# Batch 0 of a fused attention and feed-forward kernel in another layout of the accumulation banks

## Chip, cores and metric

The kernel runs on one core of a Trainium2 chip. The metric is device time in microseconds (us) of one execution. Lower is better. The time before is the median of seven executions.

The core has a matrix engine (TensorE, PE in the profile), a vector engine (VectorE, DVE), a scalar engine (ScalarE, ACT), a general engine (GpSimd, POOL) and an engine that here only issues transfers (SyncE, SP). PE writes its products into eight accumulation banks of 2 KB per partition (PSUM); DVE and ACT carry them from there to the working memory.

## Reference

```python
B, H, S, D = q.shape                     # 8, 8, 576, 64
q_d = q.reshape(B, H, S // 4, 4, D).mean(axis=3)     # k_d, v_d the same
out_up = np.repeat(sm_attn(q_d, k_d, v_d), 4, axis=2)        # full attention over 144 positions
mask = np.abs(pos[:, None] - pos[None, :]) < 4
out_local = softmax(where(mask, 0.125 * q @ k.T, -1e9)) @ v  # a band of seven keys
x = (out_up + out_local).transpose(0, 2, 1, 3).reshape(B * S, H * D)   # 4608 x 512
h = x @ w_in                                                  # 512 x 2048
g = np.where(h > 0, h, np.exp(np.minimum(h, 0)) - 1)
return g @ w_out                                              # 2048 x 512, result fp32
```

## The kernel before, in words

Each batch has eight heads, treated as four pairs (`j` = 0 to 3). The feed-forward part runs over nine blocks `t` of 512 tokens: 16 first products of four matmuls each (`mm1.t.fc`), the activation in three steps (`e` on ACT, `m` and `g` on DVE), and 16 pieces of four matmuls of the second product (`mm2.t.i`), four pieces to a bank that ACT copies out (`oc`) and SP stores (`st`). A block needs the attention output of one or two batches.

Nothing is scheduled by a compiler. The string `ORDER` (lines 40 to 148) lists some 1,500 words; each word calls a function, and every engine executes its instructions in the order in which the words stand. So a word that must wait holds up all later words of its engine. The words that matter here:

- `Lq`, `Lk`, `Lv` load a pair's q, k, v on SP's queue (lines 309, 319), into ten staging buffers; `Cq`, `Ck`, `Cv` cast them to fp16 on POOL (373, 381). `Dq`, `Dk` load and cast two pairs in one transfer on POOL's queue (339), `WI` and `WO` a quarter of the weights (269, 274). `WL` (`hold`, 296) is a one-element write on POOL into a staging buffer: SP's next load waits for it, and with it for everything POOL has to do first.
- `Tq`, `Tk` turn q and k (`turn`; for batches 0 to 2 in 18 matmuls of 64 columns, line 408). `Aq`, `Ak` carry the turned tile away (434; ACT, and DVE for k of pairs 0 and 1 of batch 0); `Fq`, `Fk` add up fours on DVE (453).
- `SL` is the banded part of the scores (504), `SD` the pooled part (514); `SC` is both. `G0`, `G1` and `H0`, `H1` are the exponentials of the two parts on ACT (530, 536), one for each head; `E0`, `E1` are both. `M` multiplies with the band's mask on DVE (549).
- `VS` pools v (391) and `VD` carries that away on DVE (478). `DH` (batch 0, two halves) and `DEN` make the denominators (573); `RH` and `RC` invert them (583, 587).
- `OUT` makes a pair's output (624, 630), `LG` carries it to the working memory on ACT (645, 648), `RB` spreads the inverted denominators by ten matmuls with a selector (613), `MUL` multiplies the two on DVE (657, 660), `X` adds the two parts into the block's input, on POOL but for one on DVE (673).
- `Z` and `FILL` put matmuls of 512 columns on constant data into the next tile before its real work (254).
- `K?` loads constants; `KS` loads the selector `SEL`, 128 x 1280 fp16, on POOL's queue (211).

Until the word `Q0` only batch 0 is computed. The eight banks are then two double-bank tiles with the tag `two` and two with the tag `more`. All turns, the v sums (but one), the first half's denominators, the outputs and the spread use `two` in rotation; the scores, one v sum, the second half's denominators and one spread use `more`. A tile is handed on when its last reader is done. `SL` and `SD` of one head share a tile: the pooled scores lie behind the banded ones in the same banks (columns 288 to 431). At `Q0` the banks of `more` are given to the feed-forward part, as two banks `hp` and two banks `misc`.

Of the kernel before, what the change touches and what calls it, by code (L numbers as in the profile page):

```python
# [15 lines left out]
SD = S // 4  # L16
# [34 lines left out]
Lv1.3 e.0.2 SC1.0 e.0.1 Fk1.1 Cv1.0 mm1.0.4 E01.0 m.0.2 g.0.2 WO2 e.0.3 VS1.0 E11.0 m.0.1
mm1.0.6 VD1.0 WO3 g.0.1 e.0.4 SC1.1 WLv2.0 M1.0 e.0.6 mm1.0.9 E01.1 m.0.4 g.0.4 E11.1 m.0.6
OUT1.0 g.0.6 mm1.0.15 LG1.0 M1.1 Tq1.3 m.0.3 Tq1.2 g.0.3 Aq1.3 Dq2.1 mm1.0.14 Aq1.2 Fq1.3 Tk1.2
e.0.15 Fq1.2 mm1.0.7 e.0.14 m.0.15 Lv2.0 Ak1.2 g.0.15 Cv1.1 Tk1.3 e.0.7 Fk1.2 Dk2.1 mm1.0.8
Ak1.3 m.0.7 e.0.9 g.0.7 SC1.2 Fk1.3 E01.2 m.0.14 g.0.14 E11.2 VS1.1 m.0.9 mm1.0.13 VD1.1 e.0.8
M1.2 SC1.3 e.0.13 m.0.8 g.0.9 E01.3 m.0.13 mm1.0.5 g.0.13 E11.3 g.0.8 OUT1.1 e.0.5 M1.3 mm1.0.11
LG1.1 m.0.5 g.0.5 Tq2.0 e.0.11 Tq2.1 Cv1.2 Lv2.1 Aq2.0 mm1.0.12 Aq2.1 m.0.11 g.0.11 VS1.2 e.0.12
Tk2.0 VD1.2 mm2.0.0 Fq2.1 Ak2.0 Fq2.0 Tk2.1 OUT1.2 Fk2.0 Ak2.1 mm2.0.1 LG1.2 m.0.12 g.0.12
mm1.0.10 Fk2.1 DEN1 e.0.10 m.0.10 SC2.1 g.0.10 E02.1 RC1 mm2.0.2 E12.1 RB1.2 mm2.0.3 MUL1.2
Cv1.3 Lv2.2 RB1.1 oc.0.0 M2.1 VS1.3 st.0.0 mm2.0.4 MUL1.1 X1.2.2 X1.2.1 mm2.0.5 VD1.3 X1.1.2  # L60
X1.1.1 RB1.0 OUT1.3 MUL1.0 mm2.0.6 LG1.3 X1.0.2 Lv2.3 RB1.3 X1.0.1 Tq2.2 MUL1.3 mm2.0.7 Aq2.2
Cv2.0 Fq2.2 Tk2.2 X1.3.2 Lq3.0 oc.0.1 X1.3.1 VS2.0 Ak2.2 mm2.0.8 st.0.1 VD2.0 Cv2.1 Fk2.2 SC2.0
Lk3.0 Cv2.2 mm2.0.9 E02.0 mm2.0.10 E12.0 Tq2.3 M2.0 Tk2.3 Lv3.0 Aq2.3 mm1.1.0 Cv2.3 Ak2.3 Fq2.3
mm1.1.3 e.1.0 Fk2.3 Cq3.0 Lq3.1 SC2.2 e.1.3 m.1.0 mm2.0.11 E02.2 g.1.0 m.1.3 mm2.0.12 E12.2
g.1.3 Ck3.0 Lk3.1 mm1.1.1 oc.0.2 M2.2 st.0.2 mm1.1.4 e.1.1 m.1.1 Lv3.1 VS2.3 e.1.4 g.1.1 Cv3.0
OUT2.0 mm2.0.13 VD2.3 LG2.0 m.1.4 g.1.4 Cq3.1 Lq3.2 mm1.1.6 mm1.1.11 e.1.6 Ck3.1 Lk3.2 SC2.3
e.1.11 mm2.0.14 m.1.6 E02.3 g.1.6 mm2.0.15 m.1.11 E12.3 g.1.11 mm1.1.2 Cv3.1 Lv3.2 oc.0.3 st.0.3
mm1.1.5 M2.3 e.1.2 m.1.2 VS2.2 Lq3.3 e.1.5 g.1.2 OUT2.3 DEN2 VD2.2 LG2.3 m.1.5 g.1.5 mm1.1.9
Lk3.3 RC2 mm2.1.0 e.1.9 m.1.9 mm1.1.7 Lv3.3 g.1.9 Cv3.2 VS2.1 e.1.7 mm1.1.10 VD2.1 m.1.7 g.1.7
OUT2.1 e.1.10 Lq4.0 RB2.1 LG2.1 m.1.10 mm1.1.15 g.1.10 MUL2.1 RB2.0 e.1.15 Lk4.0 mm1.1.13 MUL2.0  # L70
X2.1.2 RB2.3 e.1.13 m.1.15 mm2.1.1 g.1.15 X2.0.2 Lv4.0 MUL2.3 OUT2.2 X2.0.3 mm1.1.8 X2.1.3 LG2.2
m.1.13 Lq4.1 g.1.13 X2.3.2 RB2.2 e.1.8 Tq3.0 MUL2.2 X2.3.3 Cv3.3 mm1.1.14 Aq3.0 m.1.8 Tk3.0
VD3.0 X2.2.2 e.1.14 g.1.8 Ak3.0 Tq3.1 X2.2.3 mm1.1.12 KD3.0 Cq3.2 Aq3.1 m.1.14 mm2.1.2 Lk4.1
e.1.12 g.1.14 Cq3.3 Tq3.2 VD3.1 Cv4.0 mm1.2.0 Aq3.2 m.1.12 g.1.12 Cq4.1 Tk3.1 e.2.0 VD3.2 Ck3.3
# [24 lines left out]
MUL4.0 mm1.3.15 X4.3.4 Lq6.3 m.3.12 SC5.2 e.3.15 g.3.12 X4.0.4 mm2.3.2 E05.2 Cv6.1 mm1.4.0 E15.2
m.3.15 g.3.15 Cv6.2 Tq5.3 e.4.0 M5.2 mm1.4.2 Aq5.3 m.4.0 g.4.0 Cq6.2 Tk5.3 e.4.2 mm2.3.3 VD5.3  # L100
X4.0.5 Ak5.3 mm1.4.3 m.4.2 oc.3.0 g.4.2 Ck6.2 st.3.0 Tq6.2 KD5.3 e.4.3 Cq6.1 mm1.4.10 Aq6.2
m.4.3 g.4.3 Cq6.0 Tk6.2 e.4.10 mm2.3.4 VD6.2 X4.3.5 Ak6.2 Lk6.3 mm2.3.5 m.4.10 g.4.10 Cv6.0
mm1.4.5 KD6.2 SC5.3 e.4.5 mm1.4.7 E05.3 m.4.5 g.4.5 mm2.3.6 E15.3 mm1.4.12 e.4.7 M5.3 SC6.2
m.4.7 e.4.12 g.4.7 DEN5 E06.2 m.4.12 g.4.12 mm1.4.14 E16.2 RC5 mm1.4.13 SO5 M6.2 e.4.14 Tq6.1
e.4.13 m.4.14 g.4.14 Tq6.0 Aq6.1 Cq6.3 mm2.3.7 Aq6.0 m.4.13 VD6.1 mm1.4.1 g.4.13 oc.3.1 VD6.0
st.3.1 Tk6.1 e.4.1 mm1.4.15 Ck6.3 SI5 mm2.3.8 m.4.1 g.4.1 Ck6.0 e.4.15 mm2.3.9 Ak6.1 Lv6.3
m.4.15 Tk6.0 g.4.15 Lq7.0 mm1.4.9 Ak6.0 Lk7.0 KD6.1 mm1.4.8 KD6.0 e.4.9 m.4.9 SC6.1 e.4.8 g.4.9
mm2.3.10 E06.1 m.4.8 g.4.8 mm1.4.4 E16.1 mm1.4.11 e.4.4 M6.1 SC6.0 m.4.4 e.4.11 g.4.4 mm2.3.11
E06.0 m.4.11 Lv7.0 g.4.11 mm2.3.12 E16.0 OUT5.1 oc.3.2 M6.0 Lq7.1 OUT5.2 st.3.2 MUL5.1 Cv6.3
mm2.3.13 Cq7.0 MUL5.2 mm1.4.6 Lk7.1 X5.1.5 OUT5.3 X5.1.6 e.4.6 OUT5.0 MUL5.3 mm2.3.14 X5.2.5  # L110
Lv7.1 X5.2.6 MUL5.0 mm2.3.15 X5.3.6 Tq6.3 Lq7.2 oc.3.3 m.4.6 g.4.6 X5.0.5 Tk6.3 Aq6.3 st.3.3
mm2.4.0 X5.0.6 Ak6.3 VD6.3 mm2.4.1 X5.3.5 KD6.3 Cv7.0 Lk7.2 SC6.3 Ck7.1 mm1.5.0 E06.3 Cq7.1
mm1.5.8 E16.3 Lv7.2 Cv7.1 Tq7.0 e.5.0 M6.3 e.5.8 Tq7.1 m.5.0 Aq7.0 Lq7.3 g.5.0 Ck7.0 DEN6 Aq7.1
# [37 lines left out]
def _np_consts():  # L151
# [15 lines left out]
    for e in range(2):  # L167
        for g in range(RN):
            sel[:, RN * e + g, g, e] = 1.0
# [640 lines left out]
```

## Time and profile before

| | |
|---|---|
| median of 7 runs | 364.0 us (362.22 to 367.38) |
| profiled execution, its own time | 366.4 us |
| its span, first to last instruction | 364.6 us |
| PE busy | 350.4 us (96% of the span) |
| DVE, ACT, POOL busy | 241.1, 208.9, 122.0 us |
| mm1 matmuls (line 681), 576 of 128 x 512 | 144.4 us busy |
| mm2 matmuls (line 725), 576 of 128 x 512 | 142.0 us busy |

The profile is of one execution, and the other six have only a time. A busy PE is not PE at its peak: a matmul's row is longer than the step from one matmul to the next. Four 128 x 512 matmuls in a row step on by 0.86 us on the chain, 0.22 us each. Where the timeline merges a group, its duration runs from the first start to the last end, and a group may begin before the one ahead of it has ended. "issue" is idle time for which the profile shows no event that ended it.

### The profile page before, as it was taken

The page shows a single profiled execution, that of the slowest core. Times are in us where ns is not written, and L with a number is a line of the kernel's source. Part 1 is how long each engine was busy: PE and PEld are TensorE (multiplying, and loading weights), DVE is VectorE, ACT ScalarE, POOL GpSimd, SP SyncE. Part 2 cuts the span into 40 slices and gives each one's busy share as a digit, 9 for nine tenths or more (in the row PEclk, how much of TensorE's full clock was granted, in tenths as well). Part 3 has the DMA queues.
Part 4 walks back from the last instruction along what each step waited for, and adds up shares of the span by engine and source line. Part 5 has one row for each costly group of instructions (what it writes and reads, how often), then busy time and mean ns, then how long its engine had stood idle before and what let it go on. Part 6 is the DMA issues. An engine that isn't in the chain of part 4 may idle for free.

```text
span 364.6 us, 9565 instructions
## 1 busy us (share of the span) xinstructions
PE 350.4 (96%) x3960; PEld 184.4 (51%) x3960; DVE 241.1 (66%) x473; ACT 208.9 (57%) x395; POOL 122.0 (33%) x177
## 2 busy tenths in 40 slices
PE   7898978999999998999999999999999999999995
PEld 3664544554565463565555655645544444444442
DVE  2878985577887575658797875868666655555520
ACT  2757884277567785376767775674743344444421
POOL 5777211562195150652193219506001400000000
PEclk9999999899999999999999999999999999999999
DMA  8999999598997998666952399940013010010012
GB/s 269 209 188 200 197 197 197 111 164 171 206 169 151 166 173 166 119 138 125 191 106 61 78 190 221 147 133 31 29 53 91 30 59 29 29 60 29 29 60 86
DMA packets 106918, 46.10 MB, mean 126 GB/s; under 512 B 92314, under 2 KB 101178, under 8 KB 106874
## 3 DMA queue, kind: packets, MB, share of 16 engines
q1 hardware_dynamic: 96586, 34.61, 47.4%
q0 software_dynamic: 6576, 6.96, 11.2%
q10 hardware_dynamic: 3712, 3.93, 5.1%
q8 instruction: 31, 0.51, 0.6%
q14 instruction: 13, 0.11, 0.1%
HBM read 42.50 MB, written 9.53 MB: 143 GB/s over the span
## 4 chain that ended last, share of the span: by engine, by line
PE 79%; DMA 14%; POOL 2%; SPq 1%; DVE 1%; ACT 1%; issue 1%; ACTq 0%
PE op L725 34%; PE hp L681 30%; DMA v<-in_v_dram 10%; PE sc L504 3%; PE lg L624 2%; DMA rd<-rc 2%; PE den L573 2%; PE tq L391 2%; PE tq L414 2%; DMA q<-in_q_dram 1%; PE tk L414 1%; PE rb L613 1%; PE lg L630 1%; SPq L319 1%; POOL WI L269 1%; POOL v L381 1%
## 5 line engine op out<-in xcount | busy, mean ns | idle before, releaser
L681 PE MATMUL hp<-xt,WI 128*128 128x512 f16 x576 | 144.4, 380 | 0.2
L725 PE MATMUL op<-WO,gt 128*128 128x512 f16 x576 | 142.0, 382 | 1.1 <-DVE gt L715 1.1
L706 ACT ACTIVATE e<-hp 128x512 f16<-128x512 f32 x144 | 85.6, 600 | 80.5 <-PE hp L681 74.7
L715 DVE SCALAR_TENSOR_TENSOR gt<-hp,e 128x512 f16<-128x512 f32 x144 | 99.1, 690 | 4.8
L725 PEld LDWEIGHTS <-gt 128*128 128x128 f16 x576 | 53.5, 98 | 62.6 <-DVE gt L715 1.6
L710 DVE TENSOR_SCALAR e<-e 128x512 f16<-128x512 f16 x144 | 49.7, 345 | 52.0 <-ACT e L706 50.5
L681 PEld LDWEIGHTS <-WI 128*128 128x128 f16 x576 | 52.9, 98 | 59.3 <-issue 0.9
L673 POOL TENSOR_TENSOR xt<-ln,gn 128x64 f16<-128x64 f16 (+7 forms) x63 | 42.3, 695 | 62.4 <-DVE ln L660 62.3
L530 ACT ACTIVATE pex<-sc 112x576 f16<-112x576 f32 x64 | 41.0, 647 | 10.9 <-PE sc L514 8.5
L381 POOL CAST v<-v 112x768 f16<-112x768 f32 x30 | 25.4, 855 | 49.3 <-DMA v<-in_v_dram 27.1
L732 ACT COPY os<-op 128x512 f32<-128x512 f32 x36 | 21.1, 586 | 31.3 <-PE op L725 30.8
L549 DVE TENSOR_TENSOR mex<-pex,MASK 112x1152 f16<-112x1152 f16 x32 | 27.6, 862 | 17.0 <-ACT pex L530 16.8
L536 ACT ACTIVATE dex<-sc 72x288 f16<-72x288 f32 x64 | 25.5, 405 | 1.3 <-PE sc L514 1.3
L376 POOL CAST k<-k 96x768 f16<-96x768 f32 x20 | 16.6, 837 | 26.0 <-issue 12.6
L376 POOL CAST q<-q 96x768 f16<-96x768 f32 x20 | 17.6, 887 | 20.4 <-issue 14.8
L504 PEld LDWEIGHTS <-kt 64*112 64x112 f16 x384 | 12.9, 127 | 14.2 <-issue 11.4
L504 PE MATMUL sc<-qt,kt 64*112 64x96 f16 x384 | 17.1, 218 | 2.0 <-issue 1.3
L439 ACT CAST qt<-tq 128x720 f16<-128x720 f32 x20 | 15.0, 763 | 5.7 <-PE tq L391 3.1
L391 PEld LDWEIGHTS <-VR 112*72 112x72 f16 x192 | 13.1, 115 | 6.3 <-issue 2.7
L660 DVE TENSOR_TENSOR ln<-lg,rcb 128x576 f16<-128x576 f32 x20 | 14.9, 747 | 0.0
L624 PEld LDWEIGHTS <-v 112*64 112x64 f16 x384 | 10.6, 109 | 7.7 <-issue 5.9
L624 PE MATMUL lg<-mex,v 112*64 112x96 f16 x384 | 13.7, 209 | 0.6 <-ACT lg L648 0.3
(65 smaller groups left out, 271.8 us busy)
## 6 DMA issues: line engine op xcount, KB each, us to landing
v<-in_v_dram SPq DMA_DIRECT2D x28, 336.0 KB, 6.8
out_dram<-os SPq DMA_DIRECT2D x36, 256.0 KB, 2.3
q<-in_q_dram SPq DMA_DIRECT2D x24, 288.0 KB, 6.2
k<-in_k_dram SPq DMA_DIRECT2D x24, 288.0 KB, 5.8
rcb<-rd ACTq DMA_DIRECT2D x10, 360.0 KB, 6.2
WI<-in_moe_w_in_dram POOLq DMA_DIRECT2D x4, 512.0 KB, 10.7
WO<-in_moe_w_out_dram POOLq DMA_DIRECT2D x4, 512.0 KB, 15.7
q<-in_q_dram POOLq DMA_DIRECT2D x4, 288.0 KB, 11.6
```

Of the source, the lines that this page charges most:

```text
L376: nc.gpsimd.tensor_copy(out=t, in_=x.rearrange("p (e c d) -> p c e d", e=2, d=D))
L381: nc.gpsimd.tensor_copy(out=t[:], in_=st32.pop(("v", b, j)).rearrange("p (e c) d -> p c e d", e=2))
L504: nc.tensor.matmul(sc[e][0:KW, c // 3, QB * (c % 3) : QB * (c % 3) + QB], kt[r, QB * c : QB * c + KW], q_of(b, j, r, c), start=True, stop= ...
L530: nc.scalar.activation(out=stS[(b, j)][2][:, e, :].rearrange("p (g u) -> p g u", g=2), in_=scs[(b, j)][e][0:KW, :, 0:HB], func=AF.Exp, sca ...
L549: nc.vector.tensor_tensor(out=mex[:], in0=pex[:], in1=mk2, op=AB.mult)
L624: nc.tensor.matmul(lg[64 * e : 64 * e + 64, c // 3, QB * (c % 3) : QB * (c % 3) + QB], v16[:, c, e, :], mex[:, e, QB * c : QB * c + QB], s ...
L673: eng.tensor_tensor(out=xts[t][:, j, t0 - TBLK * t : t1 - TBLK * t], in0=ln[:, a:z], in1=_rep4(gn[:, a // 4 : z // 4]), op=AB.add,)
L681: nc.tensor.matmul(hps[(t, fc)][:], WI[:, dc, 128 * fc : 128 * fc + 128], xts[t][:, dc, :], start=(dc == 0), stop=(dc == DMC - 1),)
L706: nc.scalar.activation(out=e[:], in_=hps[(t, fc)][:], func=AF.Exp)
L710: nc.vector.tensor_scalar(out=e[:], in0=e[:], scalar1=1.0, scalar2=-1.0, op0=AB.min, op1=AB.add)
L715: nc.vector.scalar_tensor_tensor(out=gts[t][:, fc, :], in0=hps[(t, fc)][:], scalar=0.0, op0=AB.max, in1=els.pop((t, fc))[:], op1=AB.add,)
L725: nc.tensor.matmul(ops[(t, tt)][:], gts[t][:, fc, 128 * tt : 128 * tt + 128], WO[:, fc, :], start=(fc == 0), stop=(fc == FCN - 1),)
```

## The change

The banks of batch 0 are laid out anew. In place of two double-bank tiles `more` there are four single banks with the tag `t`. Turns of batch 0 go there as fp16 (a turned pair, 576 values, then fits one bank), made with the matrix engine's transpose flag; so do the v sums, the pooled scores (each head in a bank of its own, no longer behind the banded scores) and both halves of the denominators. The double-bank tiles `two` hold the banded scores, the outputs and the spread alone.

The selector is loaded as 128 x 20 values as the first constant on POOL's queue, and the new word `KX` widens it to 128 x 1280 with two DVE copies that read each value 64 times. Before, it was loaded whole, with the word `KS` standing behind `Ck0.3`.

`ORDER` is written anew as a whole. All its words are the same but for `KX` and the `Z` words, which now stand for 21 filling matmuls in place of 20.

```diff
-RB_MORE = ((0, 2),)
+RB_MORE = ()
 ORDER = """
-KM Lq0.0 KV TBL Lk0.0 FILL Lq0.1 KN Lk0.1 KE Lq0.2 KI Lk0.2 Cq0.0 Ck0.0 Lq0.3 Tq0.0 Lk0.3 Aq0.0
-Tk0.0 Cq0.1 Lv0.0 Ak0.0 Ck0.1 Lv0.1 Z2 Tq0.1 Fq0.0 Lv0.2 SL0.0 Cq0.2 Aq0.1 Fk0.0 Ck0.2 Tk0.1
-G00.0 Z2 Tq0.2 Cq0.3 Ak0.1 G10.0 Fq0.1 Aq0.2 Ck0.3 SD0.0 Tk0.2 H00.0 Fk0.1 KS H10.0 Ak0.2 M0.0
-SL0.1 Z3 Tq0.3 Fq0.2 G00.1 Cv0.0 Lv0.3 G10.1 Fk0.2 Z3 VS0.0 Aq0.3 M0.1 Fq0.3 SD0.1 Tk0.3 Cv0.1
-H00.1 H10.1 Dq1.0 Ak0.3 SL0.2 Fk0.3 WI0 G00.2 G10.2 VD0.0 Dk1.0 Z2 VS0.1 M0.2 Cv0.2 SD0.2 VD0.1
-DH0.0 H00.2 H10.2 WI1 VS0.2 RH0.0 WI2 SL0.3 VD0.2 Z2 OUT0.0 G00.3 WI3 G10.3 RB0.0 WLv1.0 LG0.0
-Lv1.0 M0.3 SD0.3 Lv1.1 H00.3 Cv0.3 Lv1.2 MUL0.0 OUT0.1 H10.3 Z1 DH0.1 LG0.1 X0.0.1 X0.0.0 VS0.3
-RH0.1 RB0.1 VD0.3 Z2 OUT0.2 MUL0.1 Z1 RB0.2 LG0.2 X0.1.0 OUT0.3 MUL0.2 Z2 RB0.3 LG0.3 X0.1.1 Q0
...
+KM Lq0.0 KS KE Lk0.0 FILL TBL Lq0.1 KV Lk0.1 Lq0.2 KN Lk0.2 KI Cq0.0 KX Ck0.0 Lq0.3 Tq0.0 Lk0.3
+Aq0.0 Tk0.0 Cq0.1 Lv0.0 Lv0.1 Ak0.0 Z2 Tq0.1 Ck0.1 Lv0.2 Fq0.0 SL0.0 Cq0.2 Aq0.1 Fk0.0 Fq0.1
+Ck0.2 Tk0.1 G00.0 Z2 Tq0.2 Ak0.1 Cq0.3 G10.0 SD0.0 Fk0.1 Aq0.2 Tk0.2 Ck0.3 SL0.1 H00.0 Fq0.2
+Ak0.2 Z3 Tq0.3 M0.0 H10.0 G00.1 SD0.1 Fk0.2 Cv0.0 Lv0.3 Tk0.3 Aq0.3 G10.1 Fq0.3 Z3 VS0.0 H00.1
+M0.1 H10.1 Ak0.3 SL0.2 VD0.0 Cv0.1 SD0.2 G00.2 Fk0.3 DH0.0 G10.2 Z2 VS0.1 RH0.0 H00.2 Cv0.2
+H10.2 SL0.3 VD0.1 WI0 SD0.3 M0.2 Z1 VS0.2 G00.3 G10.3 Dq1.0 Z2 OUT0.0 VD0.2 H00.3 M0.3 H10.3
+RB0.0 LG0.0 Cv0.3 Z1 DH0.1 Dk1.0 MUL0.0 OUT0.1 WI1 RH0.1 Z1 VS0.3 LG0.1 X0.0.0 RB0.1 VD0.3 Z1
+OUT0.2 MUL0.1 WI2 LG0.2 OUT0.3 WI3 LG0.3 Z1 RB0.2 WLv1.0 X0.1.1 Lv1.0 X0.1.0 MUL0.2 Lv1.1 Z2
+RB0.3 Lv1.2 X0.0.1 Q0 MUL0.3 X0.2.0 Tq1.0 X0.3.0 X0.2.1 Q1 Dq1.1 Aq1.0 Fq1.0 Dk1.1 Q2 X0.3.1
+mm1.0.0 WO0 Tk1.0 e.0.0 Tq1.1 WO1 Ak1.0 mm1.0.3 m.0.0 mm1.0.1 g.0.0 mm1.0.2 Aq1.1 WO2 Tk1.1
+Fk1.0 e.0.1 mm1.0.4 WO3 e.0.2 Fq1.1 e.0.3 WLv2.0 Dk2.0 m.0.1 Ak1.1 g.0.1 Dq2.0 Fk1.1 SC1.0 e.0.4
+mm1.0.5 m.0.3 E01.0 g.0.3 E11.0 m.0.2 mm1.0.9 g.0.2 m.0.4 SC1.1 e.0.5 M1.0 mm1.0.6 Lv1.3 e.0.9
+m.0.5 E01.1 g.0.4 Cv1.0 g.0.5 E11.1 mm1.0.10 m.0.9 e.0.6 g.0.9 VS1.0 mm1.0.7 e.0.10 VD1.0 m.0.6
...
-    sel = np.zeros((NPAIR, 32, RN, 2, 64), dtype=np.float16)
-    for e in range(2):
-        for g in range(RN):
-            sel[:, RN * e + g, g, e] = 1.0
+    sel = np.zeros((NPAIR, 32, 2 * RN), dtype=np.float16)
+    for i in range(2 * RN):
+        sel[:, i, i] = 1.0
...
+    def widen():
+        t = names["SELW"] = sb.tile([128, RN, 128], FP16, tag="SELW", bufs=1, name="SELW")
+        s = at_once("SEL")[:]
+        for e in range(2):
+            nc.vector.tensor_copy(
+                out=t[:, :, 64 * e : 64 * e + 64],
+                in_=_free(s[:, RN * e : RN * e + 1], [[1, RN], [0, 64]]),
+            )
...
+    def one(name, dtype=FP32):
+        t = bank("t", name)
+        for _ in range(fillers[0]):
+            nc.tensor.matmul(t[:], BUSY[:, 0:128], BUSY[:], start=True, stop=True)
+        fillers[0] = 0
+        return t if dtype == FP32 else t[:].bitcast(FP16)
...
-            tp[(n, b, j)] = two("t" + n)
+            tp[(n, b, j)] = one("t" + n, FP16) if b == 0 else two("t" + n)
...
                         x[r, D * i : D * i + D], eye[r, :], start=True, stop=True,
+                        is_transpose=(b == 0),
...
-        x = tp[("v", b, j)] = (more if (b, j) == (0, 3) else two)("vs")[:, :, 0:128]
+        if b == 0:
+            x = one("vs")[:, 0:256].rearrange("p (g w) -> p g w", g=2)
+        else:
+            x = two("vs")[:, :, 0:128]
...
-        if b == 0:
-            scs[(b, j)] = [more("sc"), more("sc")]
+        scs[(b, j)] = [two("sc"), two("sc")]
...
+        if b == 0:
+            dns[(b, j)] = [one("sd")[:, 0 : 2 * SD].rearrange("p (g w) -> p g w", g=2) for _ in range(2)]
+        else:
+            dns[(b, j)] = [x[:, :, HB : HB + SD] for x in scs[(b, j)]]
...
-            den = dens[(b, half)] = (more if half else two)("den")[:, 0, :]
+            den = dens[(b, half)] = one("den")
...
-                rb[:, bk, a : a + RG], at_once("SEL")[r, 128 * g : 128 * g + 128], rc[r, :],
+                rb[:, bk, a : a + RG], names["SELW"][r, g], rc[r, :],
...
-    banks_as(("more", 2, 1024))
+    banks_as(("t", 4, 512))
```

Further on, the new order of PE's words up to the pooled v of pair 2 of batch 1 is: `VS1.0 mm1.0.7 OUT1.0 Tq1.3 mm1.0.12 Tq1.2 mm1.0.13 Tk1.3 mm1.0.11 Tk1.2 mm1.0.14 SC1.3 mm2.0.0 VS1.1 mm1.0.8 OUT1.1 mm2.0.1 SC1.2 mm1.0.15 mm2.0.2 DEN1 VS1.2 RB1.0 RB1.1 mm2.0.3`. Before it was, from `SC1.0` on: `SC1.0 mm1.0.4 VS1.0 mm1.0.6 SC1.1 mm1.0.9 OUT1.0 mm1.0.15 Tq1.3 Tq1.2 mm1.0.14 Tk1.2 mm1.0.7 Tk1.3 mm1.0.8 SC1.2 VS1.1 mm1.0.13 SC1.3 mm1.0.5 OUT1.1 mm1.0.11 Tq2.0 Tq2.1 mm1.0.12 VS1.2 Tk2.0 mm2.0.0 Tk2.1 OUT1.2 mm2.0.1 mm1.0.10 DEN1 SC2.1 mm2.0.2`.

## The prediction

> **What bounds the kernel now.** First the page's chain of waits, by engine, and from the chain in order of time the one long piece that is not PE's:
>
> ```profile
> PE 79%; DMA 14%; POOL 2%; SPq 1%; DVE 1%; ACT 1%; issue 1%; ACTq 0%
> ```
> ```profile
> 24.83 29.25 DMA v<-in_v_dram
> ```
>
> PE sets the end, but up to 54.08 us the chain runs through a load of v. So I cut the busy time by stage (span, then PE, PEld, DVE, ACT, POOL, granted clock, DMA share, GB/s):
>
> ```profile
> 0.00:28.18 28.18, 24.27 (x464) 15.01 (x464) 16.97 (x27) 15.38 (x31) 19.74 (x39) 1.00 1.09 221
> 28.18:62.48 34.30, 29.18 (x533) 15.88 (x530) 29.00 (x55) 24.30 (x50) 11.86 (x18) 1.00 1.20 198
> 62.48:72.94 10.46, 10.34 (x112) 5.36 (x110) 5.14 (x11) 3.82 (x8) 5.18 (x8) 0.84 0.64 120
> 72.94:347.13 274.19, 272.76 (x2799) 142.12 (x2800) 188.34 (x378) 162.51 (x301) 85.24 (x114) 1.00 0.56 111
> ```
>
> 28.18 is the first feed-forward matmul. From 72.94 on PE idles 1.4 of 274 us: nothing to win there. Until 62.48 it idles 9.0 us, with the transfer engines full. In the third row the granted clock falls; a cut at 64.06 to 67.47 gives 0.50 for 3.41 us, so 1.7 us of PE work is lost. Which waits, the timeline of PE and its neighbours says:
>
> ```profile
> 18.03 1.33 POOL L381 CAST v<-v 112x768 f16<-112x768 f32 x1
> 19.41 0.50 PE L391 MATMUL vs<-v,VR 112*72 112x128 f16 x6 [0.40 <-POOL v L381]
> 20.38 1.19 ACT L530 ACTIVATE pex<-sc 112x576 f16<-112x576 f32 x2 [1.55 <-PE sc L504]
> 36.40 0.50 PE L391 MATMUL vs<-v,VR 112*72 112x128 f16 x6 [1.11 <-POOL v L381]
> 47.24 0.53 PE L391 MATMUL vs<-v,VR 112*72 112x128 f16 x6 [1.09 <-ACT dex L536]
> 54.15 0.82 POOL L381 CAST v<-v 112x768 f16<-112x768 f32 x1 [7.43 <-DMA v<-in_v_dram]
> 55.02 0.49 PE L391 MATMUL vs<-v,VR 112*72 112x128 f16 x6 [1.15 <-POOL v L381]
> 62.17 0.25 PE L504 MATMUL sc<-qt,kt 64*112 64x96 f16 x3 [1.27 <-issue]
> ```
>
> Four v sums that stand too early in PE's order (19.41, 36.40, 47.24, 55.02), and a pause of 1.27 us inside SC2.1 that no event explains; 1.9 us after it the clock falls.
>
> **Batch 0, to 28.18.** Before, VS0.2 waits for Cv0.2, which started at 18.03 because three transfers were issued on POOL ahead of it (15.83 to 18.06); SL0.3 stands behind VS0.2, so G00.3 starts at 20.38, after 1.55 us of idle ACT. After, Cv0.2 stands ahead of these transfers and SL0.3, SD0.3 ahead of VS0.2. SD also need not wait for the exponential that reads its bank (it began at 21.74, just behind G10.3), nor SL for H. I walk the new order with the steps between starts on ACT (turn copy 0.55, G 0.57, H 0.34) from Aq0.2, at 10.83 as before: G00.1 12.6, Aq0.3 13.2, G10.1 13.7, Ak0.3 15.0, G00.2 15.5. PE then has DH0.0 (1.0), VS0.1 and two fillers, so SL0.3 stands at 17.65 and G00.3 starts at 18.2: 2.2 us earlier. Most is given back. OUT0.3 takes the tile that MUL0.1 reads until 24.65; RB0.2 and RB0.3 wait for LG0.2 (25.4) and LG0.3 (26.35), because outputs and spreads alone now rotate through two tiles. RB0.3 stands at 26.9 in place of 27.76. **0.9 us earlier**; bounds 2.2 earlier (nothing given back) and 1.2 later (v0.2 lands as late as 18.03 and the two waits stay). The one filler more (0.21) is in the walk.
>
> The turns in another mode have no row. The fp32 turns of 18 took 0.47; I take that, as the columns are the same. The far end is two cycles for one, 8 x 0.47 = 3.8, about half on the path; a gain I exclude, since 18 steps of 64 columns fill the 0.47. The Trainium skill, TensorE: Matmul & The Clock Gate, Part 4: PE-mode transpose, says that transposes in this mode do not count as busy to the clock's monitor. By it the eight turns would no longer hold the clock up, and a dip like that at 64.06, 1.7 us, could fall into batch 0; no row here has such a turn. The copies of the turns read fp16 from a bank, again without a row. I keep 0.64 (ACT) and 0.76 (DVE, two copies), as the inner step is still 64 elements; the other end is DVE's 128x512 fp16 row, 0.28 to 0.35, some 0.8 for both.
>
> KX: two DVE copies of 640 values; by L710 (0.35 for 512) 0.43 each, by the fp16 addition L673 (0.69) 0.86. Constants on POOL's queue took 4.9 to 5.4 us to land, so SEL, issued at 1.42, is there at 6.4 and Ak0.0 moves from 6.46 to between 7.3 and 8.1. It ends by 8.9; SL0.0 started at 8.94 and SD0.0 at 10.72 (Fk0.0 then ends by 10.3). Ak0.0 waits behind KX on DVE, and SL0.0 behind Ak0.0, so it is hidden: **0**; a microsecond later it would cost up to 1. SEL's issue (0.57 at 13.11) moves to POOL's first 3.98 us, ahead of the first cast, which waited 0.77 for its load. The 0.32 MB no longer moved are 1.7 us of the queue's 0.77 MB in 4 us (20 to 24), counted with the loads below.
>
> **The loads of v.** WLv1.0 now stands behind X0.0.0 and WI2, WI3 on POOL: X0.0.0 needs MUL0.0 (22.2 in the walk), so Lv1.0 goes out at 25.05 in place of 21.63. v1.0 landed at 35.5, and v1.1 and v1.2 9.7 and 8.9 later: SP's queue moved 0.85 MB against 3.06 of POOL's from 32 to 52. Bounds for v1.2: 57.5 (the whole 3.4 later) and 53 (bytes alone, SEL's gone); I take 54.8, since before, SP moved nothing from 20 to 24 anyway. WI0 (issued by 16.8, at 10.7 to landing) just makes Q0 at 27.3; WI1 (20, at 12.0) makes mm1.0.4 at 32.4.
>
> **28 to 62.** The new order puts VS1.0 five words of PE later (40.0 instead of 36.40), VS1.1 at 49.2, and VS1.2 behind the last first product, three mm2 and DEN1, at 57.1. With the landings above none waits; at the late end VS1.2 waits 1.3 (cast 0.82), with RB1.0 and all mm2 behind it on PE. So 1.11 + 1.09 + 1.15 go, a wait of 0.23 before OUT1.0, and, if it was of this order, the pause of 1.27: 4.85 in all. New waits in their place: Ak1.1 now stands behind e.0.1, e.0.2, e.0.3 on ACT (0.55 each) and ends at 34.55, while PE is through mm1.0.4 at 33.2: SC1.0 takes that tile and waits 1.4, with mm1.0.5 behind it. DEN1 stands two products (1.75) behind SC1.2, whose two E (0.95 each) and M1.2 (0.75) need 2.75: 1.1. Six more (SC1.1, mm1.0.14, VS1.1, OUT1.1, SC1.2, RB1.0) come to 1.65, each at most 0.5. Bounds 2.5 and 4.15; since groups on PE begin up to 0.4 ahead of the end of the one before, I take half of the small ones: **3.3**. DVE (29.0 of 34.3) is next behind PE.
>
> **The clock.** With fewer pauses up to 62, the dip of 1.7 goes. Cases below say what if not.
>
> **After 73.** The order is rewritten there too, with the same words. I count 0: at best 1.1 (a single pause, at 142.02), at worst the rival below.
>
> **Sum**, against the profiled 366.4 (span 364.6): -0.9 - 4.85 + 3.3 - 1.7 = -4.15, so 362.25. That execution lies 2.4 over the median; taking the difference over, 364.0 - 4.1 = **359.9**. Its own range is 357.8 (prologue 2.2, new waits 2.5) to 365.0 (prologue 1.2 later, KX 1, v1.2 1.3, new waits 4.15).
>
> **Rivals.** A measurement of this kernel can tell about 1% (3.6 us) from no change.
>
> *Pause and dip belong to no order.* The pause at 62.17 has no releaser ("issue") and falls inside a group, so what ended it may recur elsewhere and take the clock along. For it: another pause of that size (1.13, at 142.02) is inside a group of mm2 too, though there DVE's gt is named. Then 1.27 + 1.7 stay: 362.9, within 1%. The same place holds if the change doesn't do what it says, batch 0 ending when it did (360.8 to 363.8).
>
> *The rewritten order pauses PE in the long stage.* From 73 on PE has no slack, and a pause of 1.27 that trips the clock costs 1.27 + 1.7 = 3.0. Against it: 274 us of the old order held one pause and no dip, and DVE and ACT are 69% and 59% busy there. For it: each double-bank tile there is handed on by ACT or DVE, every handing-on has a new place, and SC1.0 shows how one ACT word misplaced costs 1.4. From three such places on the gain is gone and turned: 359.9 + 9 = 368.9, slower.
>
> **How the numbers follow.** Forecast 0.45 (faster), pause and dip stay 0.28 (within 1%), pauses in the long stage 0.27 (slower). The range reaches from 357.0, a little under the forecast's own, to 368.4, just short of the last rival's full price; it leaves out some 5% below and 12 to 15% above.
>
> **What would show it.** Right: G00.3 near 18.2, first mm1 near 27.3, none of VS1.0 to VS1.2 ended by a cast, SC1.0 waiting for ACT's kt (L434), a granted clock of 1.00 from 60 to 75. Wrong: a turn group over 0.5, Ak0.0 after 8.2, a v sum still waiting, or idle PE over 2 us after 73 with a clock under 1.00.

## The result, and the profile after

The changed kernel takes 368.3 us in the median of 27 executions (364.25 to 370.55), the kernel before 365.2 us in 64 beside it. The ratio is 1.0076, with a 95% interval of 1.0054 to 1.0098: about 2.8 us slower, inside the 1% named in the prediction, but beyond the scatter. The ratios in this text leave out each kernel's slow executions, those more than 1.5% above its fastest, and the medians hold all of them. 359.9 us was forecast. The execution profiled took 367.47 us; its span is 365.7 us.

The chain of waits after, by engine, and from the chain in order of time the long transfer:

```profile
PE 79%; DMA 12%; DVE 4%; POOL 3%; SPq 1%; issue 1%; ACT 0%; POOLq 0%; DVEq 0%; ACTq 0%
...
28.36 28.72 DMA v<-in_v_dram
```

The same load, v1.2, still carries the chain. It was issued at 28.36 us (before: 24.83), took about as long (28.72 us, before 29.25), and landed at 57.08 (before: 54.08). Cut by stage from the first feed-forward matmul on (span, then PE, PEld, DVE, ACT, POOL busy, granted clock, DMA share, GB/s), with two finer cuts below:

```profile
0.00:27.36 27.36, 24.16 (x465) 14.81 (x465) 17.06 (x29) 15.30 (x31) 19.54 (x38) 1.00 0.92 195
27.36:62.50 35.14, 31.40 (x475) 16.26 (x473) 28.26 (x56) 22.03 (x45) 13.37 (x21) 0.94 1.21 199
62.50:73.00 10.50, 10.50 (x158) 5.65 (x159) 4.81 (x8) 4.85 (x10) 4.13 (x6) 0.87 0.64 133
73.00:347.13 274.13, 270.53 (x2802) 140.74 (x2801) 192.41 (x379) 164.19 (x305) 83.55 (x113) 1.00 0.58 112
...
58.33:65.16 6.83, 6.83 (x59) 3.60 (x57) 3.24 (x7) 1.41 (x3) 3.25 (x5) 0.50 1.21 209
56.20:58.30 2.10, 0.29 (x6) 0.33 (x6) 0.63 (x2) 0.00 (x0) 0.83 (x1) 1.00 1.21 198
```

Three things stand here. Batch 0 ends at 27.36, as forecast (27.3). Then PE does next to nothing from 56.2 to 58.3, and from 58.33 the clock is at a half for 6.83 us: 3.4 us of PE work lost, twice the loss of before (3.41 us at a half). And in the long fourth row PE idles 3.6 us where it idled 1.4. The timeline of POOL, PE and DVE puts names to it:

```profile
57.13 0.83 POOL L399 CAST v<-v 112x768 f16<-112x768 f32 x1 [8.08 <-DMA v<-in_v_dram]
58.01 0.54 PE L409 MATMUL vs<-v,VR 112*72 112x128 f16 x6 [1.81 <-POOL v L399]
...
183.21 0.82 POOL L399 CAST v<-v 112x768 f16<-112x768 f32 x1
183.99 2.01 POOL L698 TENSOR_TENSOR xt<-ln,gn 128x256 f16<-128x256 f16 x3
183.35 2.79 DVE L735 TENSOR_SCALAR e<-e 128x512 f16<-128x512 f16 x1
186.93 1.04 PE L706 MATMUL hp<-xt,WI 128*128 128x512 f16 x4 [1.22 <-DVE gt L740]
...
255.38 2.80 DVE L735 TENSOR_SCALAR e<-e 128x512 f16<-128x512 f16 x2
258.96 1.02 PE L706 MATMUL hp<-xt,WI 128*128 128x512 f16 x4 [1.41 <-DVE gt L740]
```

The sums VS1.2 wait 1.81 us for a cast that itself waited for v1.2. At 183.35 a minimum (`m.3.12`), a DVE instruction that takes 0.29 us in the median, lasts 2.79, while POOL runs a cast and three additions without a gap; its addition `g` comes later by as much, and PE waits for it. At 255.38 the first of the two minima merged in that line (`m.5.8`) alone lasts 2.39. Counted from the end of the last matmul's step (0.22 us), and not of its longer row as in the lines above, PE's pauses there are 1.39 and 1.57 us. In before's profile no minimum of block 3 or 5 lasts over 0.75 us (the longest of all 1.14).

### The profile page after: what moved, and what is told of

It reads as the page before. It is cut to its first block, busy times and chain, and to the rows that moved or that the text cites. A ratio compares the mean times of both kernels' runs of the same rounds, so it can differ in the third digit from the quotient of the medians.

```text
span 365.7 us, 9575 instructions
## 1 busy us (share of the span) xinstructions
PE 351.5 (96%) x3961; PEld 184.0 (50%) x3961; DVE 244.4 (67%) x475; ACT 210.0 (57%) x395; POOL 120.6 (33%) x177
## 4 chain that ended last, share of the span: by engine, by line
PE 79%; DMA 12%; DVE 4%; POOL 3%; SPq 1%; issue 1%; ACT 0%; POOLq 0%; DVEq 0%; ACTq 0%
PE op L750 33%; PE hp L706 30%; DMA v<-in_v_dram 10%; PE sc L524 3%; PE lg L649 2%; DVE e L735 2%; PE tq L409 2%; PE tq L433 2%; DMA q<-in_q_dram 2%; PE tk L433 2%; PE den L598 1%; PE rb L638 1%; PE lg L655 1%; POOL v L399 1%; POOL WI L287 1%; PE sc L539 1%
## 5 line engine op out<-in xcount | busy, mean ns | idle before, releaser
L706 PE MATMUL hp<-xt,WI 128*128 128x512 f16 x576 | 141.8, 380 | 3.7 <-DVE gt L740 3.5
L735 DVE TENSOR_SCALAR e<-e 128x512 f16<-128x512 f16 x144 | 56.8, 396 | 48.2 <-ACT e L731 46.6
L698 POOL TENSOR_TENSOR xt<-ln,gn 128x64 f16<-128x64 f16 (+7 forms) x63 | 41.2, 678 | 74.7 <-DVE ln L685 46.4
L574 DVE TENSOR_TENSOR mex<-pex,MASK 112x1152 f16<-112x1152 f16 x32 | 24.3, 759 | 16.9 <-ACT pex L555 16.8
L561 ACT ACTIVATE dex<-sc 72x288 f16<-72x288 f32 x56 | 22.6, 403 | 0.0
L461 ACT CAST kt<-tk 128x576 f16<-128x576 f32 x20 | 12.8, 640 | 2.9 <-DMA out_dram<-os 1.9
```

Of the source, the lines that this page charges most:

```text
L561: nc.scalar.activation(out=stS[(b, j)][1][:, e], in_=dns[(b, j)][e][0:KG], func=AF.Exp, scale=SCALE / 16.0,)
L574: nc.vector.tensor_tensor(out=mex[:], in0=pex[:], in1=mk2, op=AB.mult)
L698: eng.tensor_tensor(out=xts[t][:, j, t0 - TBLK * t : t1 - TBLK * t], in0=ln[:, a:z], in1=_rep4(gn[:, a // 4 : z // 4]), op=AB.add,)
L706: nc.tensor.matmul(hps[(t, fc)][:], WI[:, dc, 128 * fc : 128 * fc + 128], xts[t][:, dc, :], start=(dc == 0), stop=(dc == DMC - 1),)
L735: nc.vector.tensor_scalar(out=e[:], in0=e[:], scalar1=1.0, scalar2=-1.0, op0=AB.min, op1=AB.add)
```

## Experiments

Two theories. **Late load**: v1.2 lands 3 us later, PE pauses, and the pause costs a half clock besides. **Long stage**: the rewritten order queues two minima behind divisions (`MUL`) into a row of POOL work that holds them. The rivals are that the clock falls by itself, and that these stages only look different. To compare profiles of different orders I use PE's curve: the time at which PE has done a given amount of work (every matmul but the fillers counted by its columns at full clock, some 352 us in all, the same in every kernel here), less the same time in before's profile.

**Four splices** of the two orders, cut at `Q0` and at `mm2.1.0`.

```diff
 Lv1.2 X0.0.1 Q0
-MUL0.3 X0.2.0 Tq1.0 X0.3.0 X0.2.1 Q1 Dq1.1 Aq1.0
+X0.2.1 MUL0.3 X0.2.0 Tq1.0 X0.3.0 Dq1.1 Q1 Aq1.0
...
```

Above, the changed start with before's order behind it:

> The changed layout and the new order up to the word Q0 (batch 0), the old order behind it. Late-load theory: the three loads of v that now go out 3.5 us later belong to this part, and the old order asks for VS1.2 earlier than the new one did, so PE waits there some 4 us (cast of v1.2 near 57.9, PE ready near 54), the clock falls, and the ratio to before is 1.005 to 1.012. Long-stage theory (the cost sits in the order behind 91 us): the old order has none of it, ratio 0.997 to 1.000. Layout theory (the new banks and the narrow selector cost by themselves): Q0 later than 28.2, which the profile of the changed kernel (27.36) already speaks against.

366.4 us, ratio 1.0047 [1.0015, 1.0079]. The wait came, but at another place than expected, at VS1.0:

```profile
39.26 0.82 POOL L398 CAST v<-held 112x768 f16<-112x768 f32 x1 [6.10 <-DMA held<-in_v_dram]
40.13 0.80 PE L408 MATMUL vs<-v,VR 112*72 112x128 f16 x6 [5.76 <-POOL v L398]
...
37.70:44.50 6.80, 4.37 (x29) 2.23 (x29) 3.46 (x7) 1.46 (x4) 2.33 (x4) 0.50 1.21 196
```

With its sums as early as before's, the changed start makes PE wait 5.76 us for the cast of v1.0, which waits for its load, and the clock is at a half again. All 12 executions had a mean clock of 0.991 or less. From 100 us on this kernel keeps before's order, and there its curve goes from +1.3 to -0.2: no loss.

The reverse, before's layout and order to `Q0` and the changed order behind it:

```diff
 RB0.3 LG0.3 X0.1.1 Q0
-X0.2.1 MUL0.3 X0.2.0 Tq1.0 X0.3.0 Dq1.1 Q1 Aq1.0
+MUL0.3 X0.2.0 Tq1.0 X0.3.0 X0.2.1 Q1 Dq1.1 Aq1.0
...
```

> The old layout and order up to Q0, the new order behind it (without KX). The loads of v go out at 21.6 again, so v1.2 lands near 54 while VS1.2 stands near 57.5 on PE. Late-load theory: no wait at VS1.2, no fall of the clock from 58 to 65, ratio 0.990 to 0.998. Long-stage theory: 1.003 to 1.008, with or without that wait.

364.7 us, ratio 1.0007 [0.9975, 1.0038]: between the two ranges, as both theories hold a part. 11 of 12 executions had a clock of 0.998 or more. With v early no sum waits: the curve is at -4.2 at 50 us of work, -4.7 at 100. Then the long stage gives part back (-6.5 at 170, -2.2 at 260), with the same held minimum:

```profile
179.10 2.79 DVE L710 TENSOR_SCALAR e<-e 128x512 f16<-128x512 f16 x1
```

The changed order to `mm2.1.0` with before's behind, and the reverse:

```diff
 e.1.7 m.1.4
-mm2.1.0 g.1.4 E02.2 Cv3.1 Lv3.2 mm1.1.8
+E02.2 E12.2 M2.2 g.1.4 mm1.1.11 e.1.11
...
```

> The changed kernel with its new order up to mm2.1.0 (about 91 us), the old order behind it. Late-load theory: VS1.2 waits 1.8 us and the clock falls for two windows as in the changed kernel, ratio 1.005 to 1.010. Long-stage theory: the wait is outweighed by the gains of 28 to 55, ratio 0.997 to 1.001.

371.9 us, 1.0159 [1.0103, 1.0216]. Slower than either range, and inconclusive as a size: the seam itself pauses PE for 3.02 us at 95.2, two windows of half clock follow (95.24 to 102.07), and the curve goes from about 0 at 70 us to +7.4 at 100. VS1.2 waits 1.71 us, with two such windows behind it too, as expected. Behind the seam it stays at +6.7 to the end, and no minimum there lasts over 1.2 us.

```diff
 mm1.1.9 Lk3.3 RC2
-mm2.1.0 e.1.9 m.1.9 mm1.1.7 Lv3.3 g.1.9
+e.1.9 VS2.1 m.1.9 g.1.9 VD2.1 mm1.1.7
...
```

> The kernel before with its old order up to mm2.1.0, the new order behind it. Late-load theory: 0.999 to 1.002. Long-stage theory: pauses of 0.8 to 1.6 us on PE between 91 and 347 us, where a DVE minimum (m) lasts over 2 us beside POOL's additions; ratio 1.005 to 1.009.

369.9 us, 1.0138 [1.009, 1.0186], again slower than either range. The curve is at +1.4 at 70 us, still in before's order (this profile has two windows of half clock there, before's has one), and at +2.5 at 100, the seam included. Behind it the curve goes on to +4.9, with minima of 2.79 and 2.38 us. In both kernels with before's order in the long stage they are absent, in both with the changed one they are there. PE's two pauses go with them: 1.39 and 1.57 or 1.58 us, in front of the same two products, in all seven profiles here that have the changed order there unmended.

**Wait or clock.** Eight filling matmuls ahead of the sums that wait:

```diff
 DEN1 Cv1.2 Lv2.1 RC1
+Z8
 VS1.2 RB1.0 VD1.2
```

> The changed kernel with eight filler matmuls of 512 columns (about 0.21 us each, 1.7 in all) put in PE's queue right ahead of the sums of batch 1's head pair 2, where the changed kernel waits 1.81 us for the late v and then runs at half clock from 58.33 to 65.16 us. Late-load theory: the fillers fill the wait and no more, POOL's cast still ends at about 58.0, and the two windows of half clock behind it go: clock 1.00 in the row from 60 to 66, about 3.4 us less than the changed kernel's profiled 367.5 there, and 364 to 366 in the median, because the long stage still costs its 3 us. Rival (the dip belongs to no pause, it comes and goes by itself): the half clock stands at 58 to 65 as before, and the fillers cost up to 1.7 us.

366.4 us, 1.0043 [1.001, 1.0076], a little over what was expected (364 to 366). The load is no earlier; fillers and a rest of 0.40 us take the place of the pause (timeline and stage cut):

```profile
56.38 1.90 PE L272 MATMUL vs<-busy 128*128 128x512 f16 x8
58.69 0.49 PE L409 MATMUL vs<-v,VR 112*72 112x128 f16 x6 [0.40 <-POOL v L399]
...
62.50:73.00 10.50, 10.50 (x163) 5.74 (x163) 6.12 (x11) 4.32 (x9) 5.13 (x8) 1.00 0.92 174
```

All 10 executions had a clock of 0.998 or more, against 8 of 28 of the changed kernel (the profiled one, at 0.990, is not one of the 8). Those 8 took 363.9 to 367.9 us, the other 20 took 367.5 to 370.6. So the half clock needs the pause and does not come by itself. The curve gained 2.1 us at 50 us of work.

**Away with the wait.** First the sums behind two more groups of mm2, cast and all:

```diff
-Cv1.2 Lv2.1 RC1 VS1.2 RB1.0 VD1.2 MUL1.0 RB1.1 mm2.0.3 MUL1.1 X1.0.1 OUT1.2 oc.0.0
+RC1 mm2.0.3 RB1.0 MUL1.0 RB1.1 oc.0.0 MUL1.1 st.0.0 mm2.0.4 X1.0.1 Cv1.2 Lv2.1 VS1.2 VD1.2 OUT1.2
...
```

> The changed kernel with the cast, the sums and the output product of batch 1's pair 2 behind two more groups of the first block's second product (mm2.0.3, mm2.0.4), so that PE has about 2 us of other work while the late v lands. Late-load theory: no wait for v above 0.3 us at the sums, no half clock behind it, and the time is 365 to 366.5 (ratio to before 1.000 to 1.004), since the long stage's 3 us remain. Rival (the late v only uncovers another wait): the wait goes to the pair's division or to X1.2, the curve of PE's work is within 0.5 us of the changed kernel's at 70 us, and the ratio stays at 1.007.

366.7 us, 1.0069 [1.0031, 1.0107]: missed, and my edit was why. The timelines of POOL and PE:

```profile
58.60 0.95 POOL L698 TENSOR_TENSOR xt<-ln,gn 128x448 f16<-128x448 f16 x1 [9.60 <-DVE ln L685]
59.50 0.81 POOL L399 CAST v<-v 112x768 f16<-112x768 f32 x1
...
60.37 0.49 PE L409 MATMUL vs<-v,VR 112*72 112x128 f16 x6 [1.75 <-POOL v L399]
```

I had moved the cast behind X1.0.1 on POOL, which waits for DVE's division until 58.60. The load had landed; the wait had only changed its cause, and 7 of 10 executions still lost clock. The profiled one did not: with its wait of 1.75 us the clock stayed at 1.00. So a pause of this size can cost the half clock and does not always. Once more, with the cast left in place:

```diff
-RC1 VS1.2 RB1.0 VD1.2 MUL1.0 RB1.1 mm2.0.3 MUL1.1 X1.0.1 OUT1.2 oc.0.0 RB1.2 X1.0.2 LG1.2 st.0.0
+RC1 RB1.0 MUL1.0 RB1.1 mm2.0.3 oc.0.0 st.0.0 MUL1.1 X1.0.1 X1.0.2
...
-mm2.0.4
+mm2.0.4 VS1.2 VD1.2 OUT1.2 RB1.2 LG1.2
```

> A better cut of the run with the sums behind mm2: there the cast of v1.2 had been moved behind X1.0.1 on POOL's queue too, started only at 59.5 us, and the sums waited 1.75 us for it. Here the changed kernel's cast stays where it is (57.13 us), and only PE's sums, their copy and the output product stand behind mm2.0.3 and mm2.0.4, past the landing. Late-load theory: the sums wait less than 0.3 us, no window of half clock between 55 and 66 us in most executions (clock 0.995 or better in 8 of 10), and the median is that of the kernel with early loads within 1 us: 363.5 to 365 us. Rival (the lateness only shows elsewhere, in RB1.2, MUL1.2 and X1.2 and through them in the next block): PE waits 1 us or more at mm1.1.0 or before it, clock as in the changed kernel, 366 us or more.

363.9 us, 0.9994 [0.9952, 1.0036]. v1.2 is nearly as late as in the changed kernel (its cast starts at 56.72 instead of 57.13), and PE no longer waits for it:

```profile
56.72 0.83 POOL L399 CAST v<-v 112x768 f16<-112x768 f32 x1 [8.03 <-DMA v<-in_v_dram]
...
58.60 0.50 PE L409 MATMUL vs<-v,VR 112*72 112x128 f16 x6
```

The clock was 0.998 or more in 8 of 10 executions and 0.995 in the others. The rival's wait of 1 us or more did not appear: PE's longest there is 0.71, at 56.23, for the reciprocal of the denominators.

The other way round, the loads earlier:

```diff
 DH0.1 Dk1.0
+WLv1.0 Lv1.0 Lv1.1 Lv1.2
 MUL0.0 OUT0.1
...
-RB0.2 WLv1.0 X0.1.1 Lv1.0 X0.1.0 MUL0.2 Lv1.1 Z2 RB0.3 Lv1.2 X0.0.1 Q0
+RB0.2 X0.1.1 X0.1.0 MUL0.2 Z2 RB0.3 X0.0.1 Q0
```

> The changed kernel with the three loads of batch 1's v (Lv1.0, Lv1.1, Lv1.2) issued right behind Dk1.0 instead of behind WI3 and X0.0.x, some 3.4 us earlier on SP's queue. Late-load theory: v1.2 lands about 3 us earlier (54 us instead of 57.1), no wait for v at its sums, no half clock from 58 to 65, time 364.5 to 366 (ratio 0.999 to 1.003), the long stage's 3 us remaining. Rival (the queue is full whatever the order of issue): v1.2 still lands at about 57 and the wait stays.

364.1 us, 1.0000 [0.9965, 1.0035]: the ratio as expected, the time a little under. The load of v1.2 goes out 3.9 us earlier than in the changed kernel (24.47) and lands 3.6 earlier (53.51), so the rival of the full queue falls. The sums follow DEN1 without a wait:

```profile
53.56 1.38 POOL L399 CAST v<-v 112x768 f16<-112x768 f32 x1 [5.87 <-DMA v<-in_v_dram]
55.20 0.53 PE L409 MATMUL vs<-v,VR 112*72 112x128 f16 x6
...
62.50:73.00 10.50, 10.50 (x182) 5.88 (x178) 5.83 (x10) 6.97 (x14) 5.15 (x7) 1.00 1.06 206
```

Two edits that have nothing in common but the wait give the same gain, a ratio lower by 0.008. That settles the late load.

**The long stage.** The changed kernel with two minima ahead of the divisions:

```diff
 m.3.5 g.3.5
+m.3.12 g.3.12
 X4.0.5 mm2.3.0 MUL4.3 X4.0.4 mm2.3.1 X4.1.4 MUL4.2 X4.3.4 mm1.3.15
-m.3.12
 SC5.2
-g.3.12
...
 X6.1.7
+m.5.10 g.5.10
 OUT6.2 e.5.8 OUT6.0 MUL6.2
...
 m.5.8
-m.5.10
 Tk7.3
-g.5.10
```

> The changed kernel with two pairs of DVE words moved and nothing else: the minimum and the addition of block 3's piece 12 ahead of MUL4.3 and MUL4.2 instead of behind them, and those of block 5's piece 10 ahead of MUL6.2 and MUL6.0. Long-stage theory (PE's pauses of 1.39 us at 187 and 1.57 at 259 are there because this minimum is queued behind the divisions and then stands still for 2.4 to 2.8 us beside POOL's row of additions and casts): both pauses go, the time is 2.5 to 3 us below the changed kernel's, 364.5 to 366. Second form of it (POOL's row holds any minimum, wherever it stands): the long minima turn up at the next place, pauses of the same size move by a few us, no gain. Rival (the long stage's loss has nothing to do with the minimum): the pauses stay at 187 and 259.

366.6 us, 1.0032 [0.9984, 1.008], a little over the range (the pause at the late v is still in it). Both forms of the theory were right, each at one place (DVE's timeline, then PE's):

```profile
178.07 0.68 DVE L735 TENSOR_SCALAR e<-e 128x512 f16<-128x512 f16 x1
181.51 2.44 DVE L735 TENSOR_SCALAR e<-e 128x512 f16<-128x512 f16 x1 [0.27 <-ACT e L731]
251.94 1.37 DVE L735 TENSOR_SCALAR e<-e 128x512 f16<-128x512 f16 x1
...
57.78 0.49 PE L409 MATMUL vs<-v,VR 112*72 112x128 f16 x6 [1.92 <-POOL v L399]
```

At the first, `m.3.12` ran early in 0.68 us, but the next minimum, `m.3.15`, was held for 2.44, and the curve still lost 1.1 us from 170 to 180. At the second the pause of 1.41 before the first product at 259 us is gone, and the curve loses nothing from 240 to 260 (changed kernel: 1.6). The last line is the wait for the late v; in this execution it lasts 1.92 us and again costs no clock (1.00 to the end).

So the row on POOL itself was shortened, with DVE's order left alone, on top of the early loads:

```diff
-m.3.12 SC5.2 g.3.12 Cv6.1 e.3.15
+m.3.12 SC5.2 g.3.12 e.3.15
 mm2.3.2 E05.2 X4.2.4
+Cv6.1
 m.3.15 mm1.4.0 E15.2 g.3.15
-X4.2.5 X4.3.5
...
 Cq6.3
+X4.2.5
...
 Ck6.3
+X4.3.5
```

> The kernel with the early loads (364.08 us) and three of POOL's words moved out of its row beside block 3's last minima: X4.2.5 and X4.3.5, which block 5 needs only some 35 us later, go behind casts of batch 6, and the cast Cv6.1 goes behind X4.2.4. DVE's order is untouched: m.3.12 is still queued behind MUL4.3 and MUL4.2. Theory that POOL's row of instructions without a gap holds DVE's fp16 minimum: m.3.12 shrinks from 2.79 to under 1.3 us and the pause of about 1.4 us that follows on PE shrinks by as much, 1.0 to 1.4 us less at 180 us of PE's work than with the early loads alone; 362.5 to 363.3 in the median. Rival (the minimum waits for something in DVE's own queue, such as the division's results or a buffer): it stays at 2.8 us and nothing is gained.

361.8 us, 0.9949 [0.9912, 0.9986], a little better than expected. `m.3.12` (the first line) at its old place behind the divisions, `m.3.15` after it, and POOL beside the first:

```profile
179.40 0.28 DVE L734 TENSOR_SCALAR e<-e 128x512 f16<-128x512 f16 x1
180.88 0.29 DVE L734 TENSOR_SCALAR e<-e 128x512 f16<-128x512 f16 x1 [0.47 <-ACT e L730]
...
179.56 0.63 POOL L697 TENSOR_TENSOR xt<-ln,gn 128x256 f16<-128x256 f16 x1 [0.25 <-DVE ln L684]
```

2.79 us became 0.28, by a change on POOL alone, whose work now leaves a gap of 0.25 us where the minimum starts; PE's pause there is gone. The rival of a wait in DVE's own queue falls.

With the two pairs of minima ahead as well (its file, like the last one's, is a line shorter: L734 is L735 above):

```diff
 m.3.5 g.3.5
+m.3.12 g.3.12
...
-m.3.12 SC5.2 g.3.12 e.3.15
+SC5.2 e.3.15
...
 X6.1.7
+m.5.10 g.5.10
...
-m.5.8 m.5.10 Tk7.3 g.5.10
+m.5.8 Tk7.3
```

> The same with the shorter row, and both pairs of minimum and addition ahead of the divisions as well (block 3's piece 12, block 5's piece 10). If the late loads and the two held minima are the whole of what the change loses: the pauses at about 183 and 255 us are both gone, PE's curve keeps the lead of 5.5 to 6.5 us over before's profiled run that it has at 170 us until the end, clock 1.00, and the median is 360.5 to 361.5 us, ratio 0.988 to 0.993. If other losses of the long stage matter, 362 to 363.5.

360.9 us, 0.9910 [0.9875, 0.9945], as expected: 3.3 us less than before by the ratio, 4.2 by the medians of this comparison. The chain no longer holds a transfer of v, and the stages have full clock:

```profile
PE 88%; DVE 6%; ACT 2%; DMA 1%; issue 1%; SPq 0%; POOL 0%; ACTq 0%; DVEq 0%
```
```profile
27.36:62.50 35.14, 32.67 (x518) 16.98 (x518) 28.65 (x57) 22.84 (x47) 15.08 (x23) 1.00 1.22 199
62.50:73.00 10.50, 10.50 (x182) 5.88 (x176) 5.76 (x10) 6.89 (x14) 5.55 (x8) 1.00 1.04 199
73.00:347.13 274.13, 272.35 (x2784) 141.59 (x2777) 190.21 (x380) 163.26 (x301) 80.97 (x109) 1.00 0.57 111
```

Last, the same repairs of the long stage behind before's start, without the new layout (the kernel of the second splice, and on it the edits of the last two diffs):

```diff
 m.3.5 g.3.5
+m.3.12 g.3.12
...
 X6.1.7
+m.5.10 g.5.10
```

> The same repairs of the long stage in the kernel that has before's layout and order up to the first mm1 and the changed order from there (364.67 us). It tells what the new PSUM layout of batch 0 itself is worth once nothing behind it pauses: with the early loads the changed layout reaches the first mm1 at 26.6 us, this kernel at 28.0. If that lead lasts, this kernel is 1.0 to 1.6 us slower than the one with the new layout and the same repairs, 361.8 to 362.8; if the lead is taken up by a later wait, both are within 0.5 us.

362.8 us, 0.9955 [0.9931, 0.9979]: 1.9 us more than with the new layout (1.6 by the ratios), a little more than the 1.0 to 1.6 expected, so the lead of the start lasts once nothing behind it pauses. Its size is loose, as the two intervals overlap: the profiled kernels with the changed start reach the first feed-forward matmul between 26.6 and 27.7 us, those with before's between 27.7 and 28.6.

PE's curve (us against before's profile, by PE work done):

```
work done, us           15     50    100    170    180    240    260    340
changed kernel        -0.8   -0.7   -1.2   -2.2   -0.9   +0.5   +2.1   +1.1
new start, old rest   -1.1   +1.4   +1.3   -0.2   -0.2   -0.2   -0.2   -0.2
old start, new rest   -0.2   -4.2   -4.7   -6.5   -5.1   -3.8   -2.2   -3.2
sums alone behind     -1.6   -5.4   -4.9   -6.1   -4.8   -3.3   -1.7   -2.6
early loads           -1.6   -5.5   -5.4   -6.9   -5.5   -4.2   -2.6   -3.6
early + row           -1.1   -4.9   -4.8   -6.2   -6.3   -4.9   -3.3   -4.3
early + row + minima  -1.1   -5.4   -5.5   -6.7   -6.4   -4.9   -4.9   -5.9
```

Not every step in a row is a gain or a loss of its kernel. All rows fall by 1.0 to 1.8 us between 100 and 170: before's profile pauses there, at 142.02, and the two splices with before's order at that place do not, so that pause belongs to the execution and not to the order. Between 180 and 240 and between 260 and 340 the rows with the changed order shift together, up by 1.3 to 1.5 us and down by some 1.0, without a long pause of PE between: the two orders have done different work by the same mark, and how narrow matmuls are counted shows there. So rows are to be compared with each other.

## Why the prediction was wrong

The time, 368.3 us, is just inside the range's upper end of 368.4, and that is luck: that end stood for three pauses of the long stage that cost clock, and none such came. (The forecast's own upper end adds up to 365.1, not 365.0.) The outcome fell to the case "within 1%", but not by the way told for it.

**The start was right.** The first feed-forward matmul stands at 27.36 (forecast 27.3), G00.3 at 18.77 (18.2; before 20.38). A turn in the new mode takes 205 to 206 ns an instruction on average (before: 206 for q, 196 for k), and the copies 0.64 us on ACT and 0.74 on DVE, as taken. That transposes don't count as busy in the same way (the Trainium skill, TensorE: Matmul & The Clock Gate, Part 4: PE-mode transpose) did not show: the clock is 1.00 to 27.36. Fillers stand between the turns, so no run here tests the rule itself. KX was not quite hidden: the first copy of k ended at 9.19 where I said 8.9, and SL0.0 came 0.45 us later than before, with no loss left at the first matmul.

**The step that failed first is the landing of v1.2**: "I take 54.8, since before, SP moved nothing from 20 to 24 anyway", and from it "With the landings above none waits". It landed at 57.08, near the end of 57.5 that I had put down, and used for the range but not for the sum. The load went out 3.53 us later and took 28.72 us in place of 29.25: the delay of the issue came through almost whole. The bound had a price in the text (VS1.2 waits 1.3; it waited 1.81), but not its consequence.

**The clock.** "With fewer pauses up to 62, the dip of 1.7 goes" is right as a mechanism: with no wait for v the clock was 0.998 or more in 7 of 10, 8 of 10 and 11 of 12 executions of three kernels (early loads, sums alone behind mm2, old start with new rest), against 10 of 31 of the kernel before. With the pause it is two windows of 3.41 us at a half in the changed kernel's profile, 3.4 us. The sign of that term hung on the landing. The two terms together are what the early loads win back: 0.0076 in the ratio, 2.8 us (4.2 in the medians).

**28 to 62** came out a little better than the sum, apart from it. VS1.0 and VS1.1 don't wait. The new waits I named are there and smaller: SC1.0 0.59 (forecast 1.4), DEN1 0.44 (1.1). With early loads the lead from the start to 50 us of work is 4.0 us (-5.53 less -1.57), of which 1.7 is before's dip; the sum had 3.25 (4.85 + 1.7 - 3.3).

**The second failing step is "After 73. ... I count 0"**. The curve of the changed kernel lost 1.3 us from 170 to 180 and 1.6 from 240 to 260. The rival "the rewritten order pauses PE in the long stage" had the place but not the mechanism: two pauses and not three, neither of which cost clock, made by DVE held beside POOL. Against it I had set DVE's share of 69%; that says nothing of one instruction held ten times its length. Mending the first place took 0.5% more off the ratio (1.0000 to 0.9949), the second 0.4% (to 0.9910); the intervals overlap, so the sizes rest on the curve, which shows each gain just where it was expected.

The rival "pause and dip belong to no order" falls in its half on the clock, which in every profile here falls only in or behind a pause of PE, and is open in its other half. The pause inside SC2.1 came again, at the same place, where before's order stands up to `mm2.1.0` (1.88 us, with two windows of half clock behind it), but not with that order behind the changed start, nor with the changed order in any profile here. What ends it no run shows. The pause at 142.02, named in the rival's favour, did not come again either.

Mended at these three places, the kernel stands 3.3 us (ratio) to 4.2 us (medians, 360.9 and 365.1) under the kernel before, against the 4.15 of the sum. That they agree so well is partly luck: the sum was made against before's profiled execution, and between the two profiles it is 5.9 (366.4 and 360.52). What was wrong was less the gain than that nothing would take it back: one landing and two held minima did.

## What to carry to other kernels

When an edit moves a load's issue behind other work, take its whole delay to the landing unless the trace shows the queue empty, and price the pause that follows together with the clock that it can cost: here 1.8 us of waiting brought 3.4 more in the profile, and 20 of 28 executions lost clock. When an order is rewritten, look for short DVE instructions placed beside a row of POOL work without gaps: shorten the row or move the DVE instruction, and check that the next one doesn't inherit the hold. If a repair gives nothing, look whether the wait has only changed its cause, as the cast behind X1.0.1 did.

## What the runs showed of the hardware

An fp16 minimum in SBUF (128x512) took 0.28 us alone and was held up to 2.79 us beside POOL. The divisions were not held: beside the same rows of POOL `ln` (128x576) took 0.75 us, as elsewhere. The Trainium skill, SBUF — State Buffer, "Who interferes with whom", says that DVE and GpSimd share one port pair as an exclusive lock, and that `tensor_scalar` can need it; whoever issues first blocks the other for the whole instruction. The traces agree that DVE is blocked and not slowed: the held minima of 2.79, 2.39, 2.44 and 1.37 us each end 0.15 to 0.17 us after one of POOL's instructions. By that rule alone, though, `m.3.12` would have been held to the end of the cast it met, 184.03 us; it ended at 186.15, when the three additions behind the cast were also done and POOL's next cast was already running (from 185.94). DVE can get in sooner: at 180.43 in the same profile a minimum that met an addition of such a row took 0.33 us. What decides at which of POOL's instructions DVE gets in, no run here shows. That the port is what held it was not tried by itself; that POOL's row did it was.

A pause of 1.81 us, 2.1 with little work, was enough here for two windows at half clock, each 3.41 us; in other executions 1.75 and 1.92 us cost none, and before's 1.27 us cost one. The Trainium skill, TensorE: Matmul & The Clock Gate, "Why this matters for your kernels", says to leave no idle gaps over about 3 us between bursts; here a shorter one was costly, and fillers in it kept the clock up in 10 of 10 executions.
